# Routed experts: seven of nine token blocks turned by a transposing transfer instead of on the tensor engine

## The chip, the core and the metric

The kernel runs on one core of one Trainium2 chip. The metric is the device time of one execution in microseconds (us), median of three runs: 1003.03 us before the change (1000.51 to 1003.77). The engines are named as in the profile: PE (TensorE matmuls), PEld (TensorE weight loads), DVE (VectorE), ACT (ScalarE), POOL (GpSimd) and SP (SyncE, which here only issues transfers). "Lnnn" is a line of the kernel.

## The reference

Three stages follow each other: local attention with a few global keys, a mixture of eight experts with one expert per token, and a gated feed-forward layer.

```python
x = attn_out.transpose(0, 2, 1, 3).reshape(3072, 512)
logits = x @ w_gate                       # 3072 x 8
expert_idx = argmax(logits, axis=1)
gate_w = softmax(logits)[arange(N), expert_idx]
for e in range(8):
    mask = expert_idx == e
    h = maximum(x[mask] @ w1[e], 0)       # 512 -> 1024
    out[mask] = gate_w[mask, None] * (h @ w2[e])
gate = sigmoid(out @ g_gate); val = out @ g_val
return (gate * val) @ g_out               # 512 -> 1536 -> 512
```

## The kernel before, in words

Every float32 product is made of three float16 products: each factor is split into a high half (rounded to float16) and a low half (the rest), and high x high, high x low and low x high are added up in float32.

The attention stage writes each token's row and its gate value (the sum's reciprocal, `RR`, fed by `EP` at L766) to the array `xd` in device memory, 513 float32 per row. The expert stage works on nine **items**, `ITEMS` at L41: items 0 and 1 are two blocks of 256 tokens of the fullest expert, items 2 to 8 are one block each of the other seven experts, of 480, 448, 416, 400, 384, 368 and 352 tokens. Each item has eight **steps** (`steps` at L1211, one per 128 of the 1024 hidden columns). A step of item i issues, in program order: the preparation of the next item's rows, the splitting of one block of expert weights (`wsplit`, high half on ACT at L1059, low half on DVE at L1064), the load of weights some steps ahead (`wload`, L1050, 512 KB on SP's queue), the first product of the next step (`mm1`, 12 matmuls, L1127) with its result's split (`hhigh` on ACT, L1137, `hlow` on DVE, L1141), then the **preparation of the third stage's weights** (`Prep`: ACT L964 and DVE L965, L966, L973, with loads at L941 and L947 and a store at L985, all on SP's queue, in the first 3 to 6 steps of items 1 to 7), and last the second product of this step (`mm2`, 12 matmuls, L1196). The order on each engine is the order of these calls: nothing is moved by a scheduler, and each queue is served in order.

The rows of item i+1 reach the matmuls in these steps. POOL gathers 128 rows at a time from `xd` by an index list (`gather`, L1078), in step 6 of item i-1. `xgate` (L1092, ACT) multiplies a row block by its gate values into a float32 tile `xg`, from step 1 of item i on, one block per step. `xprep` (L1143) follows two steps later, from step 3 on (`px = 3`): four PE transposes of 128 x 128 float32 into a PSUM bank (`xturn`, L1101), the high half from PSUM on ACT, scaled by `XS` (`xhigh`, L1112), the low half on DVE (`xlow`, L1116). There are four blocks for items 2 to 5 and three for items 6 to 8, 25 in all. `xT[i+1]` is read first by `mm1` of step 0 of item i+1, which is issued in step 7 of item i. Tiles `xT` alternate between two pools; `xg` has three buffers; the raw tile of `Prep` has two.

Of the kernel before, what the change touches and what calls it, by code (L numbers as in the profile page):

```python
# [8 lines left out]
F32 = mybir.dt.float32  # L9
FR = mybir.dt.float32r  # L10
F16 = mybir.dt.float16
I32 = mybir.dt.int32
U32 = mybir.dt.uint32
AF = mybir.ActivationFunctionType
ALU = mybir.AluOpType
# [4 lines left out]
DM = H * D  # L20
# [5 lines left out]
KD = DM // 128  # L26
# [7 lines left out]
EPS = 1e-9  # L34
# [6 lines left out]
ITEMS = [  # L41
    (0, 0, 256), (0, 256, 256), (1, 0, 480), (2, 0, 448), (3, 0, 416),
    (4, 0, 400), (5, 0, 384), (6, 0, 368), (7, 0, 352),
]
NIT = len(ITEMS)
# [20 lines left out]
XS = 2.0 ** 8  # L66
# [416 lines left out]
def attention(ctx, tc, g):  # L483
    nc = tc.nc
# [15 lines left out]
    moe = g.moe  # L500
# [4 lines left out]
    qn, kn, vn, qT, V = {}, {}, {}, {}, {}  # L505
    xr, xT, chain = {}, {}, {}
# [214 lines left out]
    ev = lambda t, op: nc.vector if t == NTILE - 1 or UNIT[op] == "D" else nc.gpsimd  # L721
# [43 lines left out]

    def EP(bank, t):  # L766
        chain[t]["ep"] = small(t, "ep", 1)
        ev(t, "EP").tensor_scalar(chain[t]["ep"], g.lall[:, t : t + 1], EPS, 1.0, op0=ALU.add, op1=ALU.mult)

    def SI(bank, t):  # L770
        c = chain[t]
# [233 lines left out]
class Moe:  # L1005
# [16 lines left out]
        pools.append(self.exs.enter_context(self.tc.tile_pool(name=f"{kind}{len(pools)}", bufs=n, side="right")))  # L1022

    def acts(self, i):
        return [self.xa[i % 2].tile([128, KD, 512], F16, tag=f"x{z}", name=f"xT{z}") for z in range(2)]

    def iload(self, i):
        r, c0, n = ITEMS[i]
# [65 lines left out]
    def xturn(self, i, j, b):  # L1094
        r, c0, n = ITEMS[i]
        if j == 0:
            self.xT[i] = [x[:, :, 0:n] for x in self.acts(i)]
        x = self.xg.pop((i, j))
        bk = self.g.ps.tile([128, 512], F32, tag=f"b{b}", name="mxt")
        for k in range(KD):  # L1100
            self.tc.nc.tensor.transpose(  # L1101
                bk[:, k * 128 : (k + 1) * 128], x[:, k * 128 : (k + 1) * 128], self.g.ident
            )
        w = min(128, n - 128 * j)
        self.xp[i, j] = (
            bk.rearrange("p (k n) -> p k n", k=KD)[:, :, 0:w],
            [z[:, :, 128 * j : 128 * j + w] for z in self.xT[i]],
        )

    def xhigh(self, i, j):  # L1110
        src, (xh, xl) = self.xp[i, j]
        self.tc.nc.scalar.activation(xh, src, AF.Copy, scale=XS)  # L1112

    def xlow(self, i, j):
        src, (xh, xl) = self.xp.pop((i, j))
        self.tc.nc.vector.scalar_tensor_tensor(xl, src, XS, xh, op0=ALU.mult, op1=ALU.subtract)  # L1116

    def mm1(self, i, f, b):
        n = ITEMS[i][2]
# [19 lines left out]
    def hlow(self, i, f):  # L1139
        hh, hl = self.hs[i, f]  # L1140
        self.tc.nc.vector.scalar_tensor_tensor(hl, self.hp.pop((i, f)), 0.0, hh, op0=ALU.max, op1=ALU.subtract)  # L1141

    def xprep(self, i, j):  # L1143
        self.xturn(i, j, 6 + j % 2)
# [5 lines left out]
def ffn(ctx, tc, g):  # L1150
    nc = tc.nc
    ds = bass.ds
    moe = g.moe
# [13 lines left out]
    nj = [-(-n // 128) for r, c0, n in ITEMS]  # L1167
# [43 lines left out]
    steps = [(i, f) for i in range(NIT) for f in range(NF)]  # L1211
    for n, (i, f) in enumerate(steps):
        p = (n + 1) // 2
        px = 3
        if n == 2 * NF:
            kps.close()
        if 0 < i < NIT - 1 and px <= f < px + nj[i + 1]:
            moe.xprep(i + 1, f - px)
        z = f % 2
        w = p + 1 - z  # L1220
        if NF + 4 <= n < NF + 8:
# [5 lines left out]
        w = p + 3 - z  # L1227
        if 2 < w < NP or 2 * NP + 2 < w:
            moe.wload(z, w)
        if 0 < i < NIT - 1 and px - 2 <= f < px - 2 + nj[i + 1]:  # L1230
            moe.xgate(i + 1, f - px + 2)
        prep.finish()
        if i == NIT - 1 and f > 5:
            m2.asplit(0, f - 6)
# [540 lines left out]
def spill(ctx, tc, g):  # L1775

    nc = tc.nc
    ds = bass.ds
    p = ctx.enter_context(tc.tile_pool(name="sp", bufs=1))
    V = nc.vector  # L1780
# [41 lines left out]
    x = p.tile([128, ROW], F32, name="x")  # L1822
    y = p.tile([128, DM], F32, name="y")
    idx = p.tile([1, 128], I32, name="idx")
    n = nc.values_load(num[0:1, 0:1], min_val=0, max_val=SPILL)
    with tc.For_i(0, n, 1) as i:
# [4 lines left out]
            row = nc.values_load(idx[0:1, ds(r, 1)], min_val=0, max_val=NT)  # L1831
            nc.sync.dma_start(out=g.srow[ds(r, 1), :], in_=g.xd[ds(row, 1), :])
        nc.sync.dma_start(out=x, in_=g.srow)
        V.tensor_scalar(y, x[:, 0:DM], x[:, DM : DM + 1], None, op0=ALU.mult)
        do.turn(do.xT, y)
        V.tensor_copy(y, do.expert(e))
        V.tensor_copy(y, do.gated(y))
# [216 lines left out]
```

## Time and profile before

| | |
|---|---|
| median of three runs | 1003.03 us |
| the profiled execution: device time | 993.32 us |
| its span, first to last instruction | 991.3 us |
| PE busy | 960.6 us, 97% of the span |
| DVE busy | 735.0 us, 74% |
| ACT busy | 517.8 us, 52% |
| expert stage with items 1 to 7 | about 224 to 456 us of the span |

"Busy" is the time in which an engine ran something; matmuls overlap, so a busy PE is a PE that never ran dry. In the views of stretches each engine's busy time is followed by its number of instructions; then come the granted clock of TensorE (1.00 is full), the mean busy share of the 16 transfer engines, and GB/s moved. That share can read a little over 1 in short stretches.

### The profile page before, as it was taken

How to read it: one execution, taken by the hardware profiler on the slowest of the kernel's cores; microseconds unless marked ns; L12 is line 12 of the kernel's file. 1: busy time of each engine (PE TensorE's matmuls, PEld its weight loads, DVE VectorE, ACT ScalarE, POOL GpSimd, SP SyncE). 2: the span in 40 equal slices, each digit the busy share in tenths (PEclk: the TensorE clock that was granted, in tenths of full speed). 3: DMA queues.
4: the chain of work that ended last, by engine and by line, in shares of the span. 5: the costliest groups of instructions: out<-in, count | busy, mean ns of one | idle time of the engine just before them, and what ended most of it. 6: DMA issues, size and time to landing. Idle time of an engine off the chain costs nothing.

```text
span 991.3 us, 20600 instructions
## 1 busy us (share of the span) xinstructions
PE 960.6 (97%) x7793; PEld 678.6 (68%) x7794; DVE 735.0 (74%) x1623; ACT 517.8 (52%) x993; POOL 424.2 (43%) x525
## 2 busy tenths in 40 slices
PE   6999998899999999999999999999999999999997
PEld 5888886788555556666555588666886668866686
DVE  5999999966678788876877698444984449744496
ACT  6999997845555656665544453222532226212250
POOL 8789986731344243344787812215022150221102
PEclk9999998999999999999999999999999999999999
DMA  9989867259898999996676635452355523555122
GB/s 190 203 193 186 203 143 208 78 162 296 252 306 264 319 328 296 312 332 228 176 263 244 219 125 227 171 206 102 102 228 170 197 101 105 234 176 183 38 97 100
DMA packets 165699, 197.33 MB, mean 199 GB/s; under 512 B 88547, under 2 KB 129910, under 8 KB 165590
## 3 DMA queue, kind: packets, MB, share of 16 engines
q1 hardware_dynamic: 159702, 181.72, 59.6%
q0 software_dynamic: 5008, 14.11, 4.3%
q8 instruction: 63, 1.03, 0.4%
q14 instruction: 46, 0.38, 0.1%
q10 hardware_dynamic: 880, 0.09, 0.1%
HBM read 146.81 MB, written 49.23 MB: 198 GB/s over the span
## 4 chain that ended last, share of the span: by engine, by line
PE 46%; DVE 5%; issue 3%; DMA 1%; ACT 0%; POOL 0%; POOLq 0%; DVEq 0%; SPq 0%
PE q L1400 30%; PE p L1485 12%; PE e L1508 1%; DVE h L1378 1%; DVE wk L1390 1%; PE acc L1196 1%; PE hp L1127 1%; DMA raw<-in_moe_w_gate_dram 1%; DVE wl L1064 1%; DVE yo L1320 1%; DMA raw<-yT 1%; DVE h L1447 0%; DVE h L1433 0%; DVE u L966 0%; ACT yo L1319 0%
## 5 line engine op out<-in xcount | busy, mean ns | idle before, releaser
L1400 PE MATMUL q<-yo,set 128*128 128x384 f16 x2016 | 330.2, 326 | 1.8 <-DVE h L1447 1.8
L1400 PEld LDWEIGHTS <-set 128*128 128x128 f16 x2016 | 197.2, 98 | 133.6 <-issue 4.3
L1485 PE MATMUL p<-wy,wk 128*128 128x256 f16 x1404 | 154.1, 273 | 0.1
L1485 PEld LDWEIGHTS <-wk 128*128 128x128 f16 x1404 | 137.3, 98 | 16.7 <-DVE wk L1387 0.4
L1127 PE MATMUL hp<-xT,wh 128*128 128x256 f16 (+7 forms) x576 | 135.1, 321 | 0.4 <-DVE sl L764 0.3
L1451 POOL TENSOR_TENSOR h<-h,t 128x384 f32<-128x384 f32 x60 | 59.1, 998 | 151.0 <-DVE t L1447 136.0
L1421 ACT ACTIVATE u<-q 128x384 f32<-128x384 f32 x48 | 23.1, 482 | 161.0 <-PE q L1400 161.0
L1568 POOL DMA_INDIRECT out_dram<-o,idt x24 | 23.5, 979 | 177.2 <-DVE o L1536 123.0
L1127 PE MATMUL hp<-xT,wl 128*128 128x256 f16 (+7 forms) x288 | 92.6, 322 | 2.2 <-DVE wl L1064 2.1
L1064 DVE SCALAR_TENSOR_TENSOR wl<-wr,wh 128x1024 f16<-128x1024 f32 x64 | 84.7, 1323 | 13.4 <-ACT wh L1059 12.9
L1453 ACT ACTIVATE h<-h 128x384 f32<-128x384 f32 x72 | 37.6, 522 | 102.3 <-DVE h L1447 72.7
L1196 PE MATMUL acc<-hh,wh 128*128 128x256 f16 (+7 forms) x272 | 88.2, 324 | 0.0
L1196 PE MATMUL acc<-hl,wh 128*128 128x256 f16 (+7 forms) x272 | 88.2, 324 | 0.0
L1196 PE MATMUL acc<-hh,wl 128*128 128x256 f16 (+7 forms) x272 | 88.2, 324 | 0.0
L605 ACT ACTIVATE pp<-tt,mall 128x232 f32<-128x232 f32 (+1 forms) x192 | 79.7, 480 | 1.5 <-DVE mall L588 1.5
L1196 PEld LDWEIGHTS <-wh 128*128 128x128 f16 x576 | 56.3, 98 | 34.8
L1127 PEld LDWEIGHTS <-wh 128*128 128x128 f16 x576 | 56.3, 98 | 31.5 <-issue 0.4
L1423 DVE TENSOR_TENSOR u<-q,u 128x384 f32<-128x384 f32 x48 | 26.8, 557 | 67.7 <-PE q L1400 67.7
L1137 ACT ACTIVATE hh<-hp 128x256 f16<-128x256 f32 (+7 forms) x68 | 32.9, 484 | 73.6 <-PE hp L1127 73.5
L588 DVE CUSTOM_DVE_ANT_0 tt<-s,nb 128x232 f32<-128x232 f32 (+1 forms) x192 | 66.3, 368 | 6.2 <-PE s L578 5.6
L1059 ACT ACTIVATE wh<-wr 128x1024 f16<-128x1024 f32 x62 | 64.8, 1048 | 2.4 <-DMA wr<-in_moe_w_dram 2.4
L1141 DVE SCALAR_TENSOR_TENSOR hl<-hp,hh 128x256 f16<-128x256 f32 (+7 forms) x68 | 37.3, 550 | 38.1 <-ACT hh L1137 37.9
(223 smaller groups left out, 1922.0 us busy)
## 6 DMA issues: line engine op xcount, KB each, us to landing
wr<-in_moe_w_dram SPq DMA_DIRECT2D x64, 512.0 KB, 6.3
set<-us SPq DMA_DIRECT2D x36, 896.0 KB, 5.0
wy<-wz SPq DMA_DIRECT2D x28, 768.0 KB, 5.3
us<-set SPq DMA_DIRECT2D x12, 896.0 KB, 6.1
kn<-in_k_dram SPq DMA_DIRECT2D x24, 256.0 KB, 5.6
qn<-in_q_dram SPq DMA_DIRECT2D x24, 256.0 KB, 5.3
vn<-in_v_dram SPq DMA_DIRECT2D x24, 256.0 KB, 4.5
raw<-in_moe_w_gate_dram SPq DMA_DIRECT2D x12, 512.0 KB, 7.1
```

Source lines behind the costliest of these rows:

```text
L588: nc.vector.tensor_tensor_reduce(out=tt[s][:, j, :w], in0=S_[s][j % 2][:, j // 2, :w], in1=g.nb[w][:, h, :], scale=-0.125, scalar=3.0e38, ...
L605: nc.scalar.activation(pp[s][:, j, 256 - w :], tt[s][:, j, :w], AF.Exp, bias=g.mall[:, t, h : h + 1], scale=-1.0)
L1059: self.tc.nc.scalar.activation(hi, raw, AF.Copy, scale=WS[z])
L1064: self.tc.nc.vector.scalar_tensor_tensor(lo, self.raws.pop((z, p)), WS[z], hi, op0=ALU.mult, op1=ALU.subtract)
L1127: self.tc.nc.tensor.matmul(bk, a[:, k, fs], b[:, k, :], start=(m == 0), stop=(m == 11))
L1137: self.tc.nc.scalar.activation(x[0], self.hp[i, f], AF.Relu)
L1141: self.tc.nc.vector.scalar_tensor_tensor(hl, self.hp.pop((i, f)), 0.0, hh, op0=ALU.max, op1=ALU.subtract)
L1196: nc.tensor.matmul(acc[i][dk], a[:, f % 2, d], b, start=(f == 0 and m == 0), stop=(f == NF - 1 and m == 2))
L1400: nc.tensor.matmul(bk, w[:, za, a, us], self.y[zy][:, y, u, :], start=(start and n == 0), stop=(n == 5), skip_group_check=not start,)
L1451: (V if last else G).tensor_tensor(at(half, tok), at(half, tok), d, op=ALU.mult)
L1453: A.activation(d, d, AF.Sigmoid, scale=1.0 / (YS * AS[0]))
L1485: nc.tensor.matmul(bks[t], w[:, za, j, 128 * t : 128 * t + 128], y[:, j, zy, :], start=(new and j == 0 and m == 0 and t != 1), stop=(j == ...
```

## The change

The gate's `EP` now divides by `XS`, so that the gate value itself carries the scale (exact, a power of two), and the other places that used `XS` drop it. For items 2 to 8 `xgate` and `xprep` are replaced. `rsplit` multiplies the gathered rows by the gate and splits them **by token**, before any turning: high half on ACT, low half on DVE, both into one float16 tile of 128 tokens x (512 high, 512 low) values, which takes the place of the float32 `xg` tile. `rturn` then issues **one transposing transfer** on SP's queue, from that tile straight into the `xT` tile: eight blocks of 128 features, of which each of 128 partitions receives w tokens (w is 128, or what is left of the item). The two `xT` tiles of an item become one tile with two halves. `px` goes from 3 to 2: `rsplit` runs in steps 1 to 4 (or 3), `rturn` in steps 2 to 5 (or 4), each one at the head of the step. Items 0 and 1 are turned on PE as before.

```diff
     def EP(bank, t):
-        ev(t, "EP").tensor_scalar(chain[t]["ep"], g.lall[:, t : t + 1], EPS, 1.0, op0=ALU.add, op1=ALU.mult)
+        ev(t, "EP").tensor_scalar(chain[t]["ep"], g.lall[:, t : t + 1], EPS, 1.0 / XS, op0=ALU.add, op1=ALU.mult)
...
     def acts(self, i):
-        return [self.xa[i % 2].tile([128, KD, 512], F16, tag=f"x{z}", name=f"xT{z}") for z in range(2)]
+        return self.xa[i % 2].tile([128, 2, KD, 512], F16, tag="x", name="xT")
...
+    def rsplit(self, i, j):
+        x = self.rows.pop((i, j))
+        nc, gate = self.tc.nc, x[:, DM : DM + 1]
+        y = self.xg[i, j] = self.mr[0].tile([128, DM], F32, tag="xg", name="xg").bitcast(F16)
+        hi, lo = y[:, 0:DM], y[:, DM : 2 * DM]
+        nc.scalar.activation(hi, x[:, 0:DM], AF.Copy, scale=gate)
+        nc.vector.scalar_tensor_tensor(lo, x[:, 0:DM], gate, hi, op0=ALU.mult, op1=ALU.subtract)
+
+    def rturn(self, i, j):
+        n = ITEMS[i][2]
+        if j == 0:
+            self.xA = self.acts(i)
+            self.xT[i] = [self.xA[:, z, :, 0:n] for z in range(2)]
+        w = min(128, n - 128 * j)
+        self.tc.nc.sync.dma_start(
+            out=self.xA.rearrange("p z k n -> p (z k) n")[:, :, 128 * j : 128 * j + w],
+            in_=self.xg.pop((i, j))[0:w, :], transpose=True,
+        )
...
-        px = 3
+        px = 2
...
         if 0 < i < NIT - 1 and px <= f < px + nj[i + 1]:
-            moe.xprep(i + 1, f - px)
+            moe.rturn(i + 1, f - px)
+        if 0 < i < NIT - 1 and px - 1 <= f < px - 1 + nj[i + 1]:
+            moe.rsplit(i + 1, f - px + 1)
...
-        if 0 < i < NIT - 1 and px - 2 <= f < px - 2 + nj[i + 1]:
-            moe.xgate(i + 1, f - px + 2)
```

How the instructions move shows at three places. On PE, at the head of step 3 of item 5 (400 tokens), the order before; `mxt` is the PSUM bank that takes the four turned blocks, `hp` and `acc` are the results of the first and the second product:

```order
L1196 MATMUL acc<-hh,wh_7100 128x400
L1196 LDWEIGHTS wh_7100
L1196 MATMUL acc<-hl,wh_7100 128x400
L1196 LDWEIGHTS wl_7101
L1196 MATMUL acc<-hh,wl_7101 128x400
L1101 MATMUL mxt<-ident,xg 128x128 x4
L1127 LDWEIGHTS wh_7150
L1127 MATMUL hp<-xT_6776,wh_7150 128x400
```

and the same place as it now stands:

```order
L1216 MATMUL acc<-hh,wh_7017 128x400
L1216 LDWEIGHTS wh_7017
L1216 MATMUL acc<-hl,wh_7017 128x400
L1216 LDWEIGHTS wl_7018
L1216 MATMUL acc<-hh,wl_7018 128x400
L1128 LDWEIGHTS wh_7070
L1128 MATMUL hp<-xT,wh_7070 128x400
```

The four transposes are gone, here and at the head of 24 other steps; nothing else on PE moves.

On SP's queue, steps 2 and 3 of item 5 before, behind the last load of step 1, which is the first row (`raw` is the raw tile of the third stage's weights, `wr` that of expert weights, `up` the store of prepared weights):

```order
L941 DMA raw<-in_moe_w_gate_dram 128x4x256
L1050 ISA
L1050 DMA wr_7154<-in_moe_w_dram 128x4x256
L985 DMA up_66<-u 128x512
L941 DMA raw<-in_moe_w_val_dram 128x4x256
L1050 ISA
L1050 DMA wr_7211<-in_moe_w_dram 128x2x512
L985 DMA up_66<-u 128x512
L947 DMA raw<-in_moe_w_out_dram 128x1024
```

and as they now stand:

```order
L941 DMA raw<-in_moe_w_gate_dram 128x4x256
L1158 DMA_TRANSPOSE xT<-xg 128x8x128
L1050 ISA
L1050 DMA wr_7074<-in_moe_w_dram 128x4x256
L985 DMA up_66<-u 128x512
L941 DMA raw<-in_moe_w_val_dram 128x4x256
L1158 DMA_TRANSPOSE xT<-xg 128x8x128
L1050 ISA
L1050 DMA wr_7124<-in_moe_w_dram 128x2x512
L985 DMA up_66<-u 128x512
L947 DMA raw<-in_moe_w_out_dram 128x1024
```

Each of these steps has one transfer more, ahead of the expert weights, of the store and of the next raw load; the others keep their order.

On DVE, item 5 from the end of step 0 to step 1 as it now stands (`hl` is the low half of the first product's result; `v`, `u` and `pair` are prepared weights, `wl` the low half of expert weights):

```order
L1142 SCALAR_TENSOR_TENSOR hl<-hp,hh 128x400
L965 TENSOR_SCALAR v<-raw 128x512
L966 SCALAR_TENSOR_TENSOR u<-u,v 128x512
L973 SCALAR_TENSOR_TENSOR pair<-raw,u 128x512
L1150 SCALAR_TENSOR_TENSOR xg<-x,xg 128x512
L1064 SCALAR_TENSOR_TENSOR wl_7018<-wr_6831,wh_7017 128x1024
L1142 SCALAR_TENSOR_TENSOR hl<-hp,hh 128x400
```

The split of the rows (L1150) stands ahead of the weights' split, where the low half from PSUM (L1116) stood, two steps earlier in the item.

## Rows read from the trace of the kernel before

**Rows 1.** The page's part 1: busy time, share of the span, instructions.
```profile
PE 960.6 (97%) x7793; PEld 678.6 (68%) x7794; DVE 735.0 (74%) x1623; ACT 517.8 (52%) x993; POOL 424.2 (43%) x525
```
**Rows 2.** Busy by stretch, items 1 to 7, then the stage: length, engines, clock, share, GB/s.
```profile
224.74:247.00 22.26, 22.26 (x196) 19.13 (x194) 15.04 (x25) 13.65 (x24) 2.61 (x3) 1.00 0.99 322
247.00:287.00 40.00, 40.00 (x208) 20.49 (x207) 26.80 (x40) 20.82 (x34) 15.94 (x15) 1.00 0.85 262
287.00:324.00 37.00, 37.00 (x204) 20.17 (x203) 28.71 (x39) 21.98 (x35) 13.76 (x12) 1.00 0.92 290
324.00:358.00 34.00, 34.00 (x201) 19.79 (x200) 29.18 (x40) 21.75 (x35) 11.99 (x11) 1.00 0.94 307
358.00:391.00 33.00, 33.00 (x200) 19.70 (x199) 28.39 (x39) 21.46 (x34) 12.64 (x12) 1.00 0.98 320
391.00:423.00 32.00, 31.58 (x199) 19.43 (x197) 27.10 (x36) 19.98 (x33) 10.67 (x9) 1.00 0.99 310
423.00:453.00 30.00, 29.93 (x196) 19.11 (x194) 23.24 (x33) 18.81 (x31) 13.15 (x11) 1.00 0.87 289
...
224.00:456.00 232.00, 231.51 (x1420) 140.36 (x1418) 179.81 (x250) 139.88 (x227) 81.47 (x69) 1.00 0.93 296
```
**Rows 3.** Timeline of PE in item 3: start, length, instruction.
```profile
301.24 0.60 PE L1101 MATMUL mxt<-ident,xg 128*128 128x128 f32 x4
301.67 0.54 PE L1127 MATMUL hp<-xT,wh 128*128 128x448 f16 x2
```
**Rows 4.** Groups by line and shape, 224 to 456 us: busy, mean ns, idle before.
```profile
L1064 DVE SCALAR_TENSOR_TENSOR wl<-wr,wh 128x1024 f16<-128x1024 f32 x50 | 64.0, 1281 | 7.1 <-ACT wh L1059 6.6 <-DMA up<-u 0.3
...
L966 DVE SCALAR_TENSOR_TENSOR u<-u,v 128x512 uint32<-128x512 uint32 x36 | 25.9, 720 | 4.6 <-ACT u L964 1.1 <-ACT xg L1092 0.5
...
L965 DVE TENSOR_SCALAR v<-raw 128x512 uint32<-128x512 uint32 x36 | 19.0, 529 | 2.8 <-DMA raw<-in_moe_w_gate_dram 1.6 <-DMA raw<-in_moe_w_val_dram 1.2
...
L973 DVE SCALAR_TENSOR_TENSOR u<-raw,u 128x512 uint32<-128x512 uint32 x24 | 17.4, 727 | 0.8
...
L1116 DVE SCALAR_TENSOR_TENSOR xT<-mxt,xT 128x512 f16<-128x512 f32 x19 | 13.0, 684 | 1.2 <-ACT xT L1112 1.1
...
L1112 ACT ACTIVATE xT<-mxt 128x512 f16<-128x512 f32 x19 | 11.3, 593 | 16.6 <-PE mxt L1101 16.6
...
L1141 DVE SCALAR_TENSOR_TENSOR hl<-hp,hh 128x400 f16<-128x400 f32 x8 | 4.6, 570 | 3.1 <-ACT hh L1137 3.1
```
**Rows 5.** Waits of PE, SP and ACT, 225 to 455 us: us in total, times, longest.
```profile
PE hp L1127 <- DVE wl L1064: 0.4, 1, 0.4
...
SPq L947 <- DVE u L973: 32.6, 12, 5.1
...
ACT u L964 <- DMA raw<-in_moe_w_val_dram: 3.3, 4, 2.4
```
**Rows 6.** Timelines of ACT and SP in items 5 and 6.
```profile
363.58 0.67 ACT L964 ACTIVATE u<-raw 128x512 f32<-128x512 f32 x1
366.20 0.37 SPq L941 DMA_DIRECT2D raw<-in_moe_w_val_dram  x1
367.64 0.67 ACT L964 ACTIVATE u<-raw 128x512 f32<-128x512 f32 x1
372.07 0.69 ACT L964 ACTIVATE u<-raw 128x512 f32<-128x512 f32 x1 [0.27 <-DMA raw<-in_moe_w_val_dram]
390.44 3.24 SPq L1050 DMA_DIRECT2D wr<-in_moe_w_dram  x1
407.52 0.69 ACT L964 ACTIVATE u<-raw 128x512 f32<-128x512 f32 x1 [2.42 <-DMA raw<-in_moe_w_val_dram]
```
**Rows 7.** Raw loads of L941, 225 to 456 us: issue to landing.
```profile
DMA to landing us min/median/max: 4.2/5.3/7.1
```
**Rows 8.** Busy by stretch: the busiest 4 us of the stage; a stretch of attention.
```profile
428.00:432.00 4.00, 4.00 (x28) 2.54 (x26) 3.23 (x5) 3.08 (x5) 0.00 (x0) 1.00 1.08 397
25.00:50.00 25.00, 23.66 (x325) 20.06 (x323) 23.66 (x103) 23.53 (x59) 17.81 (x28) 1.00 0.93 201
```

More of the change, by code (lines that the diff above doesn't have):

```diff
@@ L1096, in xturn @@
         if j == 0:
-            self.xT[i] = [x[:, :, 0:n] for x in self.acts(i)]
+            x_ = self.acts(i)
+            self.xT[i] = [x_[:, z, :, 0:n] for z in range(2)]
         x = self.xg.pop((i, j))
@@ L1111, in xhigh @@
         src, (xh, xl) = self.xp[i, j]
-        self.tc.nc.scalar.activation(xh, src, AF.Copy, scale=XS)
+        self.tc.nc.scalar.activation(xh, src, AF.Copy)
     def xlow(self, i, j):
         src, (xh, xl) = self.xp.pop((i, j))
-        self.tc.nc.vector.scalar_tensor_tensor(xl, src, XS, xh, op0=ALU.mult, op1=ALU.subtract)
+        self.tc.nc.vector.scalar_tensor_tensor(xl, src, 1.0, xh, op0=ALU.mult, op1=ALU.subtract)
     def mm1(self, i, f, b):
@@ L1833, in spill @@
         nc.sync.dma_start(out=x, in_=g.srow)
-        V.tensor_scalar(y, x[:, 0:DM], x[:, DM : DM + 1], None, op0=ALU.mult)
+        V.tensor_scalar(y, x[:, 0:DM], x[:, DM : DM + 1], 1.0 / XS, op0=ALU.mult, op1=ALU.mult)
         do.turn(do.xT, y)
```

## Prediction

> **What bounds the kernel now.** I read the busy times first, then the expert stage by item, then a timeline of PE, then the waits. PE is busy 97% of the span [rows 1]. In the stretches of items 1 to 7, where the change lies, PE misses 0.49 us of 228.26 us, and the 16 transfer engines show a share of 0.85 to 0.99 at 262 to 322 GB/s [rows 2]: the reader is to see there one engine that sets the pace, and a second resource close behind it. The timeline shows what the change takes away: four transposes start at 301.24 and the next product at 301.67, so a block costs PE 0.43 us [rows 3]. The 0.60 us beside them is their overlapped length, not their price. The waits show that PE waited only 0.4 us for DVE; SP waits long for DVE before a raw load; ACT is the engine that stands waiting for a raw load [rows 5].
>
> **PE.** 25 blocks x 0.43 us = 10.75 us come off the path that sets the end, 1.72 us in each of items 1 to 4 and 1.29 us in items 5 to 7. The stage could not gain more by this change.
>
> **ACT.** The copy from PSUM (19 full blocks at 0.593 us, six shorter ones) goes, and the multiplication by the gate becomes the high half of about the same size. ACT was not the bound and had waited 16.6 us for the transposes [rows 4]; worth nothing on the path.
>
> **DVE.** The low half from PSUM took 0.684 us [rows 4]. The new one reads two tiles outside PSUM; the nearest row is the weights' low half, 1.281 us for twice the elements, so 0.64 us. Bounds: 0 gain, and 0.2 us more a block (5 us in all) if it is disturbed like the worst of its neighbours. I take no change. A loaded step of DVE then still holds 1.281 + 0.570 + 0.529 + 0.720 + 0.727 + 0.64 = 4.47 us [rows 4], where a step of item 5 on PE takes 4.06 us (the raw tiles of its first two steps are taken up 4.06 us apart [rows 6]). So in items 5 to 7 DVE falls behind by some 0.4 us a step for three or four steps. Its busy time over an item, 28.39 us of 33 [rows 2], leaves room to catch up, in the steps without weight preparation. I charge nothing, but the cover is thin.
>
> **SP.** 25 issues more. Bounds per issue: 0.37 us like a raw load, 3.24 us like the longest one shown [rows 6]. SP waits 32.6 / 12 = 2.7 us for DVE ahead of an L947 load [rows 5], and the issue fits into that wait except at its upper end; behind it stand the expert weights (wanted four steps later) and the next raw load, which waits for DVE anyway. I take 0.4 us, hidden.
>
> **The transfers.** Items 2 to 8 have 2848 tokens; at 2 KB each that is 5.83 MB, 22.25 full blocks. The stage moves 296 GB/s at a share of 0.93 [rows 2], and its busiest 4 us show 397 GB/s at 1.08 [rows 8]. Taking 1.08 for full, an item needs (stretch x share / 1.08) of transfer time now: 20.4, 31.5, 31.5, 29.6, 29.9, 29.3 and 24.2 us for items 1 to 7. No row shows a transposing transfer. Bounds for a full block of 262 KB: 0.66 us at 397 GB/s; 1.30 us at the 201 GB/s of the attention stage, whose loads of q, k and v are cut into runs of 64 float32, the same 256 bytes that 128 tokens make in a row of `xT` [rows 8]. Far above lies a transfer that writes pieces an eighth as long at that row's time per piece: 10.4 us. I take 1.0 us, midway between the two near rows, since long and short runs both occur in it (1 KB in, 256 bytes out). An item then takes the longer of PE (stretch less its transposes) and transfers (need plus 3.75, 3.5, 3.25, 3.125, 3.0, 2.875 and 2.75 blocks x 1.0):
>
> item 1: PE 20.5, transfers 24.1; item 2: 38.3, 35.0; item 3: 35.3, 34.7; item 4: 32.3, 32.7; item 5: 31.7, 32.9; item 6: 30.7, 32.2; item 7: 28.7, 26.9.
>
> The longer ones add up to 224.2 us against 228.3 now: **4.1 us less**. The same sum is 220.6 (7.7 less) at 0.66 us, 228.5 (none) at 1.30, 240.9 (12.6 more) at 2.0 and 252.1 (24 more) at 2.5.
>
> The Trainium skill's "DMA: Bandwidth & Descriptors", section "Latency and other measured facts", gives 261 GB/s for one kernel's transposing transfers and 350 to 400 for contiguous ones. By the first, estimated from that page, a block takes 1.0 us and the sum stays as it is; by the second it comes near the lower bound. No run here shows either.
>
> **Landing.** `rsplit` of the last block stands in step 4, its transfer at the head of step 5, and `mm1` wants it in step 7. The nearest row is a raw load: 4.2 to 7.1 us, median 5.3 [rows 7]. Two steps are 8.1 us in item 5, less about 2 us until SP gets there: enough. In item 1 they are short, 22.26 / 8 = 2.8 us each [rows 2], so the last block can come 0 to 3 us late, and the fourth split can wait about as long for the first of three `xg` buffers. Item 1 is already charged 1.8 us for its transfers; I add nothing, and keep 3 us for the range. What is late next is the raw load: ACT takes it up 8.49 us before it takes the one that replaced it (363.58 to 372.07), the load goes out 2.62 us into that, and ACT already waited 0.27 us there and 2.42 us in item 6 [rows 6]. A block queued ahead of each raw load makes this worse; it is the way in which full transfers reach PE.
>
> The sum, -4.1, is made against the profiled execution's 993.32 us, giving 989.2; this execution is 9.71 us below the median of the runs, so against the median it is 1003.03 - 4.1, about **999.0 us**.
>
> **Rivals.** (1) *The transfers fill up what PE gives back.* A price of 1.15 to 1.4 us does it; the time is 1003 us. For it: a share of 0.98 and 0.99 in items 5 and 6, with waits for raw loads there already [rows 2, 6]. Against it: items 2 and 3 have room at any near price. (2) *The raw loads become the bound: slower.* From 1.5 us a block on, items 1 and 3 to 6 are set by their transfers; ACT stands at L964 behind a late load, `hhigh` stands behind it, and PE waits at the second product. At 2.0 us a block it is 1003.0 + 12.6, about 1016 us. For it: no stage of this kernel has less room on its transfer engines and nothing shows that turning is as cheap as copying. Against it: two or more steps of each item prepare no weights, and a late raw load can catch up there. (3) *A transposing transfer is of another order.* At 10.4 us a block it adds 22.25 x 10.4 = 231 us of transfer time, of which the stage's free 32 us (232 x 0.15 / 1.08) can take some: about 1200 us. Beside this stands the Trainium skill's "VectorE: DVE Perf Modes", section "The three transpose paths": 390 ns for a 128 x 128 square on TensorE, 1309 ns by a transfer, and the advice to use TensorE where a result in PSUM will do. Eight squares in a row would by that estimate be 10.5 us a block; the traces here show 0.11 us a square on PE and nothing on the other path. (4) *The change does nothing on PE*, because PE would only wait for DVE instead: that is seen in items 5 to 7 alone, costs at most 3 x 1.29 = 3.9 us of the gain, and lies inside the range.
>
> **How the numbers follow.** About 0.3%, 3 us, is what a measurement of this kernel can tell from no change. My forecast, with prices up to about 1.1 us and gains of 3 to 10.75 us, has a chance of 0.43; rival 1 has 0.20; rival 2, up to 2.5 us a block, 0.25; rival 3, with all above that, 0.12. So faster 0.43, same 0.20, slower 0.37. The forecast's own range is 992 to 1000. The range for all reaches from 991 (all of PE's 10.75 us, and 1 us of scatter) to 1027 (2.5 us a block), and leaves out rival 3 and little else.
>
> **What would show it.** Right: the stage of items 1 to 7 shorter by about 4 us; no transposes of `xg` beyond 16 instructions; the transposing transfers landing within 5 to 7 us; PE idle at `hp` in item 1 at most. Rival 1: PE busy falling by 11 us with idle of the same size. Rival 2: ACT L964 waiting longer for raw loads, landings of 8 us and more, and PE waiting for `hl`. Rival 3: SP's issue of a block or its landing above 10 us. The forecast is wrong if PE waits for `xT` itself, if SP is held by the issue for longer than its wait for DVE, or if transposing slows the transfers around it.

## The result, and the profile after

The changed kernel takes **1015.63 us** (median of 4 runs, 1011.49 to 1018.6) against 1002.0 us of the kernel before on the same chip: a ratio of **1.0132, 95% interval 1.0091 to 1.0174**. It is slower by some 13 us. The experiments below ran on several chips, on which the kernel before took 993.9 to 1002.3 us; so each is given as its ratio to the kernel before, measured beside it, with its 95% interval, and 0.1% is 1 us.

The page's busy times of the changed kernel (profiled execution 1016.4 us), to be held against [rows 1]:

```profile
PE 959.0 (95%) x7693; PEld 667.5 (66%) x7694; DVE 747.1 (74%) x1623; ACT 506.8 (50%) x968; POOL 422.9 (42%) x525
```

PE has 100 instructions less and hardly less busy time, and the share falls from 97 to 95%: PE waits instead of turning. The two profiled executions are 23 us apart (993.32 and 1016.4 us), of which 7 us lie ahead of the stage (it begins at 224.01 and at 230.98), so stretches are compared and not spans. To see where PE waits, I cut both traces at the store of each item's result, a fixed place of the program. The view by stretches of the kernel before, items 1 to 7 (columns as in [rows 2]):

```profile
224.01:248.03 24.02, 24.02 (x209) 20.37 (x207) 16.00 (x27) 14.03 (x25) 3.34 (x4) 1.00 0.95 308
248.03:288.60 40.57, 40.57 (x211) 20.73 (x210) 26.76 (x38) 21.83 (x35) 15.21 (x14) 1.00 0.86 268
288.60:326.47 37.87, 37.87 (x210) 20.69 (x209) 29.63 (x40) 22.44 (x37) 13.76 (x12) 1.00 0.93 292
326.47:361.88 35.41, 35.41 (x210) 20.68 (x209) 29.05 (x40) 22.18 (x37) 12.20 (x11) 1.00 0.94 306
361.88:395.56 33.68, 33.68 (x206) 20.20 (x205) 29.26 (x39) 21.38 (x35) 13.95 (x11) 1.00 0.97 313
395.56:428.59 33.03, 32.61 (x206) 20.12 (x205) 27.53 (x36) 20.49 (x34) 12.42 (x10) 1.00 1.00 321
428.59:467.42 38.83, 38.76 (x256) 25.00 (x254) 27.52 (x38) 23.77 (x38) 13.55 (x12) 1.00 0.82 274
```

and of the changed kernel:

```profile
230.98:263.06 32.08, 25.05 (x193) 19.06 (x191) 16.68 (x27) 11.95 (x21) 4.51 (x5) 0.89 0.97 278
263.06:301.88 38.82, 38.82 (x195) 18.85 (x194) 29.37 (x38) 19.87 (x31) 13.48 (x12) 1.00 0.93 269
301.88:338.01 36.13, 36.13 (x194) 18.79 (x193) 31.67 (x40) 20.85 (x33) 14.48 (x12) 1.00 1.05 316
338.01:374.45 36.44, 34.26 (x197) 18.93 (x195) 30.86 (x41) 20.94 (x33) 12.79 (x11) 1.00 1.08 333
374.45:410.53 36.08, 33.95 (x191) 18.99 (x190) 30.33 (x39) 19.53 (x31) 13.17 (x11) 0.95 1.10 336
410.53:443.40 32.87, 31.46 (x194) 18.63 (x193) 28.65 (x36) 19.07 (x31) 11.87 (x10) 1.00 1.10 343
443.40:486.63 43.23, 38.70 (x250) 24.01 (x248) 31.51 (x38) 22.76 (x35) 14.08 (x12) 1.00 0.95 265
```

Items 2 and 3 are 1.75 and 1.74 us shorter, just the four transposes. Item 1 is 8.06 us longer, with PE idle for 7.03 us and the clock down to 0.89; items 4, 5 and 7 are 1.03, 2.40 and 4.40 us longer. (The store of item 7 stands on SP behind loads of the third stage, so the last stretch reaches into item 8.) DVE is busy about 2 us longer in each of items 2 to 4 with the same number of instructions, or one more.

What PE waited for, in its timeline of the changed kernel (the bracket is the idle time ahead, and what ended it):

```profile
256.30 0.96 PE L1128 MATMUL hp<-xT,wh 128*128 128x480 f16 x2 [4.89 <-DMA xT<-xg]
360.86 0.35 PE L1128 MATMUL hp<-xT,wl 128*128 128x416 f16 x1 [2.18 <-DVE wl L1064]
396.19 0.34 PE L1128 MATMUL hp<-xT,wl 128*128 128x400 f16 x1 [2.05 <-DVE wl L1064]
461.95 0.32 PE L1216 MATMUL acc<-hl,wh 128*128 128x368 f16 x1 [1.64 <-DVE hl L1142]
466.67 0.33 PE L1128 MATMUL hp<-xT,wl 128*128 128x368 f16 x1 [2.54 <-DVE wl L1064]
```

So there are two kinds of wait: for the turned tile itself, once, in item 1, and for DVE in items 4 to 7. A wait can cost more than its length. Soon after the one that ends at 396.19 the granted clock stood at its lower level (0.50, that is 1.2 GHz) for 3.41 us, with PE busy throughout, which is some 1.7 us more of item 5:

```profile
397.21:400.62 3.41, 3.41 (x12) 1.54 (x11) 3.38 (x4) 1.98 (x4) 1.15 (x1) 0.50 1.11 374
```

Against [rows 5], the view of waits over items 1 to 7 shows for PE and ACT:

```profile
ACT u L964 <- DMA raw<-in_moe_w_val_dram: 15.9, 8, 3.3
PE hp L1128 <- DVE wl L1064: 8.5, 6, 2.5
ACT u L964 <- DMA raw<-in_moe_w_gate_dram: 5.0, 2, 4.5
```

ACT waits longer for raw loads too. DVE's groups, against [rows 4]:

```profile
L1064 DVE SCALAR_TENSOR_TENSOR wl<-wr,wh 128x1024 f16<-128x1024 f32 x52 | 72.1, 1386 | 4.7 <-ACT wh L1059 3.9 <-DMA raw<-in_moe_w_gate_dram 0.4 <-issue 0.3
L966 DVE SCALAR_TENSOR_TENSOR u<-u,v 128x512 uint32<-128x512 uint32 x36 | 29.2, 812 | 5.1 <-ACT u L964 1.8 <-DVE v L965 0.5
L1150 DVE SCALAR_TENSOR_TENSOR xg<-x,xg 128x512 f16<-128x512 f32 x25 | 20.8, 832 | 0.4 <-ACT xg L1149 0.4
```

The new split takes 0.83 us, not 0.64, and unchanged instructions became longer: 1.386 us against 1.281, 0.812 against 0.720 (only `v` became shorter, 0.467 against 0.529). A piece of item 7 shows why. DVE:

```profile
457.75 0.69 DVE L966 SCALAR_TENSOR_TENSOR u<-u,v 128x512 uint32<-128x512 uint32 x1 [0.28 <-ACT u L964]
462.34 1.46 DVE L966 SCALAR_TENSOR_TENSOR u<-u,v 128x512 uint32<-128x512 uint32 x1
464.44 2.17 DVE L1064 SCALAR_TENSOR_TENSOR wl<-wr,wh 128x1024 f16<-128x1024 f32 x1
466.99 1.21 DVE L1064 SCALAR_TENSOR_TENSOR wl<-wr,wh 128x1024 f16<-128x1024 f32 x1
```

and GpSimd, which makes low halves of the third stage's weights by subtraction (L995), in the same time:

```profile
462.04 1.21 POOL L995 TENSOR_TENSOR parts<-pair,parts 128x512 f16<-128x512 f32 x1 [1.68 <-ACT parts L994]
463.87 1.66 POOL L995 TENSOR_TENSOR parts<-pair,parts 128x512 f16<-128x512 f32 x1 [0.62 <-ACT parts L994]
```

With nothing beside it `u` takes 0.69 us and `wl` 1.21; beside a subtraction of GpSimd 1.46 and 2.17, and PE waits for that `wl` until 466.67. I set every DVE row of the five kinds that read float32 tiles (`v`, `u`, `pair`, `wl`, `xg`) against GpSimd's rows and added up what they took beyond 0.419, 0.690, 0.690, 1.221 and 0.743 us, their lengths when GpSimd computes nothing. This **extra length** is 8.9 us over items 1 to 7 before, and 20.5 us after.

The rows also show that it is waiting, and that the order of the two starts decides. The subtractions above end at 463.25 and 465.53; `u` and `wl`, which began while they ran, end 0.55 and 1.08 us later, each 0.14 us less than its own length. So it is throughout: the instructions of DVE that began while a subtraction ran (29 before, 37 after) end 0.12 to 0.20 us less than their own length after it, and hold all of the extra length but 0.5 us before and 0.1 us after; those beside which a subtraction began later (34 and 27) hold next to none, but for one `wl` of the kernel before (0.4 us). Before, 7 of `wl`, 4 of `u` and 18 of the short `v` began behind a subtraction; after, 13 of `wl`, 14 of `u`, 3 of `xg` and 7 of `v`.

### The profile page after: what moved, and what is told of

Its sections match the earlier page's. It is cut to its first block, busy times and chain, and to the rows that moved or that the text cites. A ratio compares the mean times of both kernels' runs of the same rounds, so it can differ in the third digit from the quotient of the medians.

```text
span 1014.5 us, 20450 instructions
## 1 busy us (share of the span) xinstructions
PE 959.0 (95%) x7693; PEld 667.5 (66%) x7694; DVE 747.1 (74%) x1623; ACT 506.8 (50%) x968; POOL 422.9 (42%) x525
## 4 chain that ended last, share of the span: by engine, by line
PE 40%; DVE 8%; DMA 3%; issue 3%; ACT 1%; POOL 1%; SPq 1%; another core or an unknown queue 0%; POOLq 0%; DVEq 0%
PE q L1420 29%; PE p L1505 10%; DVE h L1398 2%; DVE wk L1410 2%; DMA raw<-in_moe_w_gate_dram 1%; DMA raw<-yT 1%; POOL raw L1364 1%; PE acc L1216 1%; DMA wr<-in_moe_w_dram 1%; PE hp L1128 1%; DVE wk L1407 1%; DVE yo L1340 0%; DVE wl L1064 0%; DVE h L1467 0%; DMA wy<-wz 0%
## 5 line engine op out<-in xcount | busy, mean ns | idle before, releaser
L1128 PE MATMUL hp<-xT,wh 128*128 128x256 f16 (+7 forms) x576 | 137.2, 325 | 5.3 <-DMA xT<-xg 4.9
L1128 PE MATMUL hp<-xT,wl 128*128 128x256 f16 (+7 forms) x288 | 93.8, 326 | 9.9 <-DVE wl L1064 9.9
L1064 DVE SCALAR_TENSOR_TENSOR wl<-wr,wh 128x1024 f16<-128x1024 f32 x64 | 89.7, 1402 | 9.8 <-ACT wh L1059 9.0
L1128 PEld LDWEIGHTS <-wh 128*128 128x128 f16 x576 | 56.6, 99 | 40.4 <-DMA raw<-in_moe_w_gate_dram 5.1
L1059 ACT ACTIVATE wh<-wr 128x1024 f16<-128x1024 f32 x62 | 64.8, 1048 | 3.6 <-DMA wr<-in_moe_w_dram 3.6
```

Of the source, the lines that this page charges most:

```text
L1059: self.tc.nc.scalar.activation(hi, raw, AF.Copy, scale=WS[z])
L1064: self.tc.nc.vector.scalar_tensor_tensor(lo, self.raws.pop((z, p)), WS[z], hi, op0=ALU.mult, op1=ALU.subtract)
L1128: self.tc.nc.tensor.matmul(bk, a[:, k, fs], b[:, k, :], start=(m == 0), stop=(m == 11))
```

## The experiments

The theories: **A**, the transfer engines' time (raw loads come late); **B**, SP's issue; **C**, DVE's work; **D**, the late last block in item 1; **F** and **G**, GpSimd beside DVE.

**No transfers.** The turned tiles are filled instead; in the second kernel only once each, for items 2 and 3.

```diff
-        self.tc.nc.sync.dma_start(out=..., in_=self.xg.pop((i, j))[0:w, :], transpose=True)
+        self.xg.pop((i, j))
+        if j == 0:                             # e_none2: and i % 2 not in self.fill
+            self.tc.nc.gpsimd.memset(self.xA, 1.0)
```

> No transposing transfers at all: the turned tile is filled with ones on GpSimd once per item, so the rows of items 2 to 8 do not enter the result; the split of the rows on ACT and DVE stays as in the changed kernel. Both the theory that the transfers of the turned blocks take the time (theory A: some 2 us of all transfer engines a block, so that raw loads come late) and the one that the issue on SP takes it (theory B) expect all of it to come back and PE's 10.75 us as well: about 992 (990 to 994). If DVE's split from two tiles outside PSUM is the cause (theory C), the time stays above 1005, with PE waiting for wl and hl as often as in the changed kernel.

> As e_none (no transposing transfers; the turned tiles hold ones, so the rows of items 2 to 8 do not enter the result), but each of the two tiles is filled once and then kept, so GpSimd fills nothing from item 3 on. Theory F (GpSimd's fills of 3.5 us slowed DVE and delayed its own work there): the split costs nothing and the time falls to 9 to 11 us below the kernel before. Theory C (DVE's split stands in the steps that also prepare the third stage's weights, and DVE is the bound of items 4 to 7 once PE is 1.3 to 1.7 us an item shorter): 1 to 4 us below the kernel before, PE waiting for wl and hl in items 4 to 7.

Measured: 0.999 (0.9977 to 1.0002) and **1.001 (0.999 to 1.0031)**. Without any transfer the kernel is no faster than before; A and B had both expected 10 us. F falls as well: the fills made no difference to the time. Items 4 to 7 of e_none2:

```profile
327.78:362.25 34.47, 33.83 (x194) 18.72 (x193) 30.47 (x40) 20.54 (x33) 13.99 (x11) 1.00 0.98 318
362.25:395.72 33.47, 32.55 (x194) 18.69 (x193) 30.32 (x39) 19.88 (x32) 13.28 (x11) 1.00 0.99 321
395.72:429.33 33.61, 31.47 (x194) 18.63 (x193) 28.55 (x36) 18.97 (x31) 12.77 (x10) 1.00 1.00 322
429.33:473.21 43.88, 40.47 (x252) 24.79 (x250) 31.74 (x38) 23.03 (x36) 14.15 (x12) 0.96 0.72 244
```

Items 1 to 5 gain 5.3 us in all; items 6 and 7, and item 7 above all, pay them back. PE's waits over items 1 to 7:

```profile
PE hp L1129 <- DVE wl L1065: 6.6, 6, 2.5
```

The extra length of DVE is 20.6 us, as in the changed kernel, with no transfer in sight.

**The split's place, and no split.** In e_none_late the split of the rows stands in steps 3 to 6; in e_bare it is gone.

```diff
-        if 0 < i < NIT - 1 and px - 1 <= f < px - 1 + nj[i + 1]:
-            moe.rsplit(i + 1, f - px + 1)
+        if 0 < i < NIT - 1 and 3 <= f < 3 + nj[i + 1]:
+            moe.rsplit(i + 1, f - 3)           # e_bare: moe.rows.pop(...) instead
```

> As e_none2, but the split of the rows stands in steps 3 to 6 (or 5) of an item, where the low half from PSUM stood in the kernel before, not in steps 1 to 4. Theory C with the place as its cause: 2 to 4 us below e_none2. Theory C with the sum of DVE's work as its cause (it is the same in both): within 1.5 us of e_none2.

> Neither transfers nor split: the gathered rows of items 2 to 8 are not used at all, and the turned tiles hold ones. It is the most that the change could ever bring. If PE alone sets the pace of items 1 to 7: 10.75 us below the kernel before. If raw loads or DVE's other work are the next bound at once: less than 7 us below it.

Measured: 1.0001 (0.9988 to 1.0014) and 0.9927 (0.9903 to 0.9952). The place does not matter. Even with the split gone only 7 us of 10.75 come out (5 to 10 by the interval), and DVE's extra length is still 20.4 us. Of that, 3.5 us are one `v` beside the single fill of a tile; 17 us stand beside subtractions, against 8.9 before and 20 in e_none2. So most of it comes with the removal of the transposes, and at most some 3 us with the new split.

**GpSimd's subtractions taken away**, from three kernels (before, e_none2, changed).

```diff
-                nc.gpsimd.tensor_tensor(x[:, o, :], x[:, a, :], x[:, b, :], op=ALU.subtract)
+                nc.gpsimd.memset(x[:, o, :], 1.0)
...
-                nc.gpsimd.tensor_tensor(lo, x[:, b : b + k, :], hi, op=ALU.subtract)
+                nc.gpsimd.memset(lo, 0.0)
```

> The kernel before, with GpSimd's subtractions on the third stage's weights (L989 and L995) replaced by fills of the same tiles, so that these parts of the third stage's weights are wrong; everything else stays. It is the reference for the next two runs. Theory G (DVE's instructions on float32 tiles run longer while GpSimd computes beside them; in the kernel before this took some 10 us of DVE in items 1 to 7, which PE hardly saw): 0 to 3 us below the kernel before.

> No transfers as in e_none2 (the turned tiles hold ones), and GpSimd's subtractions replaced by fills as in the run above. Theory G (what PE gave back went to DVE, whose instructions stood beside GpSimd's for twice as long, 20 us of extra length instead of 10): 6 to 9 us below the run above. Theory C without GpSimd (DVE's own work is the bound): within 3 us of the run above.

> The changed kernel with GpSimd's subtractions replaced by fills. What is left above e_none2_nopool is the transfers' own part. Theory D with A (the late block in item 1 costs 7 to 8 us, raw loads behind the transfers some 5): 12 to 13 us above e_none2_nopool, so 4 to 6 us above the kernel before. If the transfers only did harm together with GpSimd's collisions: 8 us above e_none2_nopool, item 1 alone.

Measured: 0.9993 (0.9983 to 1.0002), **0.9893 (0.9877 to 0.991)** and 1.0063 (1.0046 to 1.008). Beside GpSimd's subtractions the removal of the transposes is worth nothing; without them it is worth 993.11 - 982.84 = 10.3 us, nearly all of PE's sum. The kernel before hardly notices them. G holds: the fills also take GpSimd less time than the subtractions, so the runs show that the subtractions are the cause, and the trace that it goes through DVE, whose extra length is 4.4 us here, not 20.6. All of the 4.4 us are one `v`, beside the fill of a turned tile by GpSimd (3.52 us from 247.72 on) and the fills behind it:

```profile
248.33 4.85 DVE L965 TENSOR_SCALAR v<-raw 128x512 uint32<-128x512 uint32 x1
```

Items 4 to 7 of e_none2_nopool have no idle PE:

```profile
320.48:354.14 33.66, 33.66 (x194) 18.80 (x193) 27.79 (x40) 20.61 (x33) 6.20 (x11) 1.00 0.99 325
354.14:386.51 32.37, 32.37 (x194) 18.79 (x193) 26.95 (x39) 19.86 (x32) 6.09 (x11) 1.00 1.02 338
386.51:417.64 31.13, 31.13 (x194) 18.80 (x193) 25.05 (x36) 19.10 (x31) 4.96 (x9) 1.00 1.02 346
417.64:455.87 38.23, 38.23 (x251) 24.32 (x249) 28.34 (x38) 23.19 (x36) 5.17 (x7) 1.00 0.78 265
```

The transfers' own part is 1.0063 - 0.9893, 17 us, without GpSimd beside them, and 1.0132 - 1.001, 12 us, with it: more than D with A said, so they do harm by themselves. The parts are thus no fixed sums: each is smaller where the other has already made PE wait.

**Where the last block lands.** e_rest_turned turns item 2 on PE again; e_item1_early keeps its transfers and puts split and transfer one step earlier in item 1 alone.

```diff
-        px = 2
+        px = 1 if i == 1 else 2                # e_item1_early
```

> Item 2, which is prepared in the short steps of item 1, is turned on PE again; items 3 to 8 are turned by transfers. Theory D (the late landing of the last block in item 1, with the clock drop that followed it, is the largest part: item 1 took 8.05 us longer): 1015.6 - 8 = about 1007, item 1 back to 24 us. Theory A alone, with the price of 2 us spread over all items: item 1 gives back 3.75 x 2 us less 1.7 us, about 1010. Both agree on the sign; item 1's length tells how much, and items 4 to 7 should stay 1 to 4 us longer than before by both.

> The changed kernel, with split and transfers one step earlier in item 1 alone (steps 0 to 3 and 1 to 4). Theory D (the last block of item 2 is issued too late on SP for the product that reads it, and the clock falls after the wait): item 1 falls from 32 us to 24 to 27, the time is 5 to 8 us below the changed kernel, that is 5 to 8 us above the kernel before. Theory A (item 1 is full of transfers): item 1 stays above 30 us, since the same bytes move in it.

Measured: 1.0047 (1.0031 to 1.0063) and 1.0064 (1.0041 to 1.0087): they take half of the loss away, or more, and item 1 falls from 32.08 us to 24.03 and 27.28. D holds for the larger part of item 1. SP's timeline of the changed kernel shows how the block got late:

```profile
244.59 2.16 SPq L1158 DMA_TRANSPOSE xT<-xg  x1
249.46 1.02 SPq L941 DMA_DIRECT2D raw<-in_moe_w_gate_dram  x1
250.53 2.45 SPq L1158 DMA_TRANSPOSE xT<-xg  x1
```

The last transfer stands behind a raw load that waits 1.0 us for ACT (`SPq L941 <- ACT wh L1059: 1.0, 1, 1.0` in the view of SP's waits), goes out at 250.53, and PE is at the product that reads it at 251.4. After that wait of 4.89 us the granted clock was 0.53 for 4.7 us, which is the lower level (1.2 GHz) for nearly all of them:

```profile
251.40:256.30 4.90, 0.01 (x1) 0.03 (x1) 1.19 (x2) 0.00 (x0) 1.17 (x2) 0.75 1.13 334
256.30:261.00 4.70, 4.70 (x14) 1.81 (x15) 0.00 (x0) 0.00 (x0) 3.34 (x4) 0.53 0.77 244
```

**What a transfer costs.** Plain transfers of the same bytes, in pieces of 256 bytes (e_plain) and of 2 KB (e_plain_long), and each kind alone (e_micro).

```diff
-            in_=self.xg.pop((i, j))[0:w, :], transpose=True,
+            in_=self.xg.pop((i, j)).rearrange("p (c n) -> p c n", c=2 * KD)[:, :, 0:w],
```

> Each transposing transfer is replaced by a plain transfer of the same bytes, from the same tile to the same tile, in pieces of 256 bytes on both sides, at the same place of SP's queue; what lands is not turned, so the products of items 2 to 8 are of other numbers. Theory A in the form that turning is what costs: a plain block takes 0.66 to 1.3 us of the transfer engines, so 993 to 1002, the issue on SP falls below 0.6 us. Theory A in the form that any further transfer of this size costs as much (the engines are full): about 1014, like the changed kernel. Theory B (SP's issue): the gain follows the issue time: 995 if the issue takes 0.4 us.

> Plain transfers in place of the turning ones, as in e_plain, but each partition's 2 KB as one run on both sides (the turned tiles are filled with ones once, and hold unturned rows in their first part). Theory A by the number of pieces (a 256-byte piece costs what a longer one does): the transfers' part falls to a quarter or less, 1 to 4 us above the kernel before if item 1's stall goes too. Theory D (what counts in item 1 is where the last transfer stands in SP's order, not its size): item 1 stays above 28 us, and the time 6 us or more above the kernel before.

> Nothing of the reference is computed: zeros are written, and then three rows of 12 transfers of 262 KB each go from one tile of 128 x 2 KB to others on SP's queue with nothing beside them: transposing ones, plain ones in pieces of 256 bytes, plain ones of 2 KB a partition. Theory A with turning as its price: a transposing one takes about 2 us of the transfer engines, a plain one of 256 bytes 0.7 to 1.3, one of 2 KB 0.7. Theory A by the number of pieces: the first two alike, the last at half of that or less. Theory B: the issue on SP (1.2 us and more) is longer than the transfer, and sets the pace of the first row.

Measured: 1.012 (1.0092 to 1.0148) and 1.0075 (1.0053 to 1.0098). Turning as such is not the price: plain pieces of 256 bytes cost as much. The stretches of e_micro (one execution), in the order transposing, pieces of 256 bytes, runs of 2 KB (length, DVE, POOL, clock, share, GB/s):

```profile
26.00:40.00 14.00, 0.00 (x0) 0.00 (x0) 1.00 1.00 191
58.00:70.00 12.00, 0.00 (x0) 0.00 (x0) 1.00 0.98 216
89.00:95.00 6.00, 0.00 (x0) 0.00 (x0) 1.00 1.02 377
```

262 KB at these rates are 1.37, 1.21 and 0.70 us a block, at a full share each. Issue by issue on SP:

```profile
L60 SPq DMA_TRANSPOSE xt<-y x12: 1324/1332/1349, 24.1 to 39.2; - x12
L67 SPq DMA_DIRECT2D xs<-y x12: 669/1168/1194, 56.6 to 68.5; - x12
L73 SPq DMA_DIRECT2D xl<-y x12: 471/606/693, 87.1 to 94.5; - x12
```

The first row does not tell whether the transfer engines or SP set its pace: its issues follow each other at 1.33 us from the first one on, which is the length of the transfers. Their landing stays at 3.2 to 3.5 us. The first three issues of pieces of 256 bytes take about 0.7 us and the others 1.17, while the landing grows from 3.1 to 4.5 us, so there the engines set it.

22.25 blocks are 30.5, 26.9 and 15.6 us at these prices, and the three kernels stand 12.2, 11.0 and 6.5 us above e_none2 (the intervals leave 3 us either way). The stretches tell where. Item 1 of e_plain and of e_plain_long:

```profile
223.80:255.67 31.87, 24.43 (x193) 18.89 (x191) 16.73 (x27) 11.98 (x21) 4.51 (x5) 0.89 0.95 280
224.90:251.75 26.85, 22.74 (x193) 18.60 (x191) 16.61 (x27) 11.96 (x21) 3.44 (x4) 1.00 0.93 312
```

Against the 23.34 us of e_none2, item 1 is 8.7, 8.5 and 3.5 us longer; items 2 to 7 together are 3.2, 2.9 and 3.4 us longer. In item 1 the cost goes with the engines' time, as A has it: at half of it PE waits 2.42 us for the turned tile, not 5.25, and the clock does not fall. Behind item 1 the cost is the same at 0.70 us a block as at 1.37, so there A by the engines' time is not shown, and why the transfers cost anything there stays open. (In e_rest_turned and e_item1_early, where item 1 has no such wait for the turned tile, items 2 to 7 lie 5.6 us above e_none2.) Of the expectations for e_plain_long, neither 1 to 4 us above the kernel before (by the pieces) nor more than 28 us in item 1 (by D) came.

**SP's queue.** Item 2 on PE as in e_rest_turned; the transfers behind the raw load of the step, or on ACT's queue.

```diff
         elif f < PREP[i] + (2 if i == 1 else 0):
             prep.start()
             prep.load()
+        if 0 < i < NIT - 1 and turned and px - 1 <= f < px - 1 + nj[i + 1]:
+            moe.rturn(i + 1, f - px + 1)       # e_rest_behind, not at the head of the next step
```

> Item 2 on PE as in e_rest_turned; for items 3 to 8 each transfer is issued at the end of the step that splits its rows, behind that step's raw load, not at the head of the next step ahead of it. If raw loads come late because a transfer stands ahead of them in SP's queue: 2 to 4 us less than e_rest_turned, so 0 to 3 us above the kernel before. If it is the engines' time (the bytes move all the same): within 1.5 us of e_rest_turned, 4 to 6 us above the kernel before.

> As e_rest_turned, but the transposing transfers of items 3 to 8 are issued by ACT on its own queue. Theory B (SP's issue of 1.2 to 3.9 us holds SP's queue and makes raw loads late): 2 to 4 us less than e_rest_turned. Engines' time: no gain; and each issue now holds ACT for as long, in front of the high halves, so 0 to 5 us more than e_rest_turned.

Measured: 1.0045 (1.0029 to 1.006), the same as e_rest_turned, and 1.0098 (1.0078 to 1.0118). Standing ahead of raw loads is not the cause. On ACT each issue holds that engine (1.16 to 1.87 us), so the second run does not clear SP by itself; that e_plain, whose issues in the kernel took 0.62 us in the median against 1.32, stands 1 us below the changed kernel, with overlapping intervals, leaves little for B.

**Versions that keep the result.** Items 3 and 4 turned (e_two_turned); items 3 to 5, with the split of the weights ahead of that of the rows (e_three_order); items 3 to 5, with GpSimd's subtractions in steps 6 and 7 (e_three_defer), and with the transfers a step earlier as well (e_three_defer_early).

```diff
-        if self.late:
+        for _ in range(min(self.quota, len(self.late))):
             self.late.pop(0)()
...
+        prep.quota = {1: 1, 6: 2, 7: 2}.get(f, 0) if 1 < i < NIT - 2 else 1
         prep.finish()
```

> Only items 3 and 4, prepared in items 2 and 3, are turned by transfers, the others on PE. In the profile of the changed kernel items 2 and 3 were 1.75 and 1.74 us shorter, each just PE's four transposes. Theory A, by which only stretches with room on the transfer engines gain (shares of 0.85 and 0.92 there): 1002.0 - 3.5 = about 998.5. A theory by which a transposing transfer disturbs the kernel wherever it runs (SP's issue, or DVE's split, theories B and C): 1002 or more.

> Items 3 to 5, prepared in items 2 to 4, are turned by transfers, the others on PE; the split of the rows stands behind the split of the weights in its step, so that DVE is already in wl when GpSimd's subtractions begin, as in the kernel before. Theory G: 3 to 5 us below the kernel before (three times 1.7 us, less what later items give back). If the later items give all of it back as in e_two_turned: within 1 us of the kernel before. If the collisions stay: 0 to 3 us above it.

> Items 3 to 5 are turned by transfers, the others on PE, the rows are split where the changed kernel splits them; GpSimd's four subtractions of the third stage's low halves (L995), which stood one a step in steps 2 to 5 beside the weight preparation, stand two a step in steps 6 and 7 of items 2 to 6, and their store in step 1 of the next item. Theory G: fewer of DVE's long instructions stand beside GpSimd (6 us of extra length or less, not 18), and the time is 3 to 5 us below the kernel before, faster than both kernels. If raw loads are what holds items 4 and 5: within 1 us of the kernel before.

> As e_three_defer, with split and transfers of items 3 to 5 one step earlier (steps 0 to 3 and 1 to 4 of items 2 to 4). In e_three_defer PE waited 0.71 and 3.62 us for the turned tile itself at the start of items 4 and 5, since SP, held by DVE at the raw loads, came to the last transfer late, as in item 1 of the changed kernel. If that is what was left (theory D): 3 to 5 us below the kernel before, faster than both kernels, with no wait for the turned tile. If DVE or the raw loads take it back again: within 1.5 us of the kernel before.

Measured: 0.999 (0.9976 to 1.0004), 1.0025 (1.0015 to 1.0035), 0.9993 (0.9972 to 1.0014) and 0.9994 (0.9981 to 1.0006). None beats the kernel before, where A had expected 3.5 us of the first, and G or D 3 to 5 us of the others. In the first, items 2 and 3 gained 1.74 and 1.75 us and item 4 lost 1.21 with PE behind `wl`. The order on DVE did not lower the extra length (17.6 us; 8 of `wl`, 10 of `u` and 7 of `xg` began behind a subtraction); moving the subtractions did (12.2 us), but then the turned tile came late, as PE's timeline of e_three_defer shows:

```profile
325.13 0.51 PE L1128 MATMUL hp<-xT,wh 128*128 128x416 f16 x2 [0.71 <-DMA xT<-xg]
363.64 0.67 PE L1128 MATMUL hp<-xT,wh 128*128 128x400 f16 x2 [3.62 <-DMA xT<-xg]
```

In e_three_defer_early that wait is gone, and PE waits for `wl` again (3.2 us in four waits), the longest of them:

```profile
327.86 0.35 PE L1128 MATMUL hp<-xT,wl 128*128 128x416 f16 x1 [1.74 <-DVE wl L1064]
```

## Why the prediction was wrong

**The sign was wrong**; 1015.63 us lies in the range only through rival 2, and that is luck, as the last point says. By its steps:

- **PE, 10.75 us off the path: right**, where nothing else takes it (10.3 us without GpSimd's subtractions). ACT's part, nothing, was right: PE waited 0.2 us for an ACT half.
- **"I charge nothing, but the cover is thin" (DVE): this step failed first.** With the transfers left out all of the gain is gone (e_none2 at 1.001). The bound of 0.2 us a block looked at the new instruction; what grew was the time that DVE's instructions, the old ones above all, waited for GpSimd's subtractions, by 20.5 - 8.9 = 11.6 us. Rival 4 had this mechanism, PE waiting for DVE, but capped it at 3.9 us and at items 5 to 7. The views read ahead of the prediction had the sign of it: means of 0.529 us for `v` and 0.720 for `u` [rows 4], where they take 0.42 and 0.69 alone. The Trainium skill has the rule, in "SBUF — State Buffer", section "Who interferes with whom": a VectorE instruction with two inputs in SBUF contends with a GpSimd instruction that reads SBUF, and not with one that only writes it. The traces agree for `u`, `pair`, `wl` and `xg`: `u` at 0.69 and 1.46 us, no extra length beside GpSimd's fills and gathers, and none on the old low half, whose source was PSUM (0.68 us beside a subtraction too). `v` has one input, and this rule does not speak of it; it waited for subtractions, and for fills as well (4.85 us). Why more of DVE's long instructions begin behind a subtraction once PE is faster was not settled: neither the place of the split (e_none_late) nor the order on DVE (e_three_order) gave the time back.
- **"I add nothing, and keep 3 us" (landing): failed.** Item 1 was 8.06 us longer where the sum had 1.8: 4.89 us of wait for the turned tile, some 2 us at the lower clock, and 2.1 us of waits for `hl` and `hh`, against 1.7 us of transposes saved. The estimate let SP be 2 us late; it was later, since the transfer stands behind raw loads that themselves wait, the last of them for ACT. The block was there at 256.30, 5.8 us after its issue began.
- **The transfers: the price was too low.** 1.37 us a block alone, where I took 1.0 with 1.30 as the upper near row. The working's own sum comes to 229.6 us at 1.37, 1.4 us more than before (and to 228.1 at 1.27, which is 1.37 us at a share of 1.00 put in the sum's terms, where 1.08 is full), so this term alone would have said "no change". The sum also let every item pay by the engines' time; only item 1 did. (A row of the split tile has 2 KB, not the 1 KB of the working; no term rests on it alone.)
- **SP's issue, 0.4 us, hidden:** it took 1.3 us alone and up to 3.9 us in the kernel (a row that can hold a wait: `SPq L1158 <- PE hp L1128: 8.0, 4, 3.6` in the view of SP's waits), but was mostly hidden, as said: e_plain, with half of it, takes about the same time.
- **Rival 2 had the time, 1016 us, and a part of the cause.** Raw loads did come late (ACT waited 24.1 us for them, 5.9 before), but half of that rise came without any transfer (15.3 us in e_none2), and the block took 1.37 us, not 2.0. It met the time by luck: DVE's waits and item 1's landing, which it does not have, made up the difference. Rival 3 fell: 1.37 us, not 10.4.

The parts, each from its runs and taken in this order: PE's transposes -10.3 us, DVE beside GpSimd +11, the transfers +12, of which item 1 has more than half; together +13. The first two are shown by runs with and without the subtractions. Of the transfers' part the stall of item 1 is shown; the rest, some 3 us, is measured, and its cause is open.

## What to carry to other kernels

When one engine is 97% busy, the gain of unloading it ends at the next engine's slack in the same stage; measure that ceiling first by leaving the replaced work out altogether. Before a step is charged nothing because an engine has room, compare that engine's rows of one shape with each other: one that takes 0.69 us here and 1.46 there waits for something inside its busy time, and its room is smaller than its busy share says. Then look which of the two began first. A transfer's place in a queue whose head waits for another engine can be worth as much as its length: item 1 took 32.08 us, 27.28 with the transfers a step earlier, and 26.85 with transfers of half the time.

## What the hardware showed that was not expected

A transposing transfer of 128 x 1024 float16 within SBUF runs at 191 GB/s with the engines' share at 1.00, a little below plain pieces of 256 bytes (216 GB/s) and half of runs of 2 KB (377 GB/s); its issue takes 1.33 us of SP with nothing beside it, which is as long as the transfer, and 1.16 to 1.87 us of ACT in e_rest_act. An instruction of DVE with two inputs outside PSUM that began while a subtraction ran on GpSimd ended 0.14 us (the row split 0.20 us) less than its own length after it (`u` 1.46 us for 0.69); if it began first, with one exception, or beside GpSimd's fills and gathers, it took its usual length. `v`, with one input, waited for fills as well: 4.85 us for 0.42. A wait of 4.89 us on PE was followed by 4.7 us at a granted clock of 0.53, and one of 2.05 us by 3.41 us at 0.50.
